# Coarse lag tables in two groups of eight shifts, and with that paired exponentials, weights multiplied before they are turned, and a new order

## The chip, the cores and the metric

The kernel runs on one core of one Trainium2 chip. A core has five engines that run on their own and meet only at semaphores: TensorE (PE, matmuls into PSUM), VectorE (DVE), ScalarE (ACT), GpSimd (POOL) and SyncE (SP, which here issues nearly all DMAs). Each engine works through its own list of instructions strictly in the order written. The metric is the device time of one execution in microseconds, the lower the better. It is not the span of the profile: the span runs from the first to the last instruction of the program, and some time lies around it.

## The reference, cut to what matters

```python
x = A_u                                            # [1, 2048, 512]
g = sigmoid((x * gate_w).sum(-1, keepdims=True))
# a: a state-space convolution over time, one filter of 2048 lags per channel d
dt = exp(log_dt)[:, None]
A, Bc, Cc = A_re + 1j*A_im, B_re + 1j*B_im, C_re + 1j*C_im      # [512, 128]
P = exp((dt*A)[:, :, None] * l)                    # l = 0..2047, as bf16
K = einsum("dn,dnl,dn->dl", Cc, P, dt*Bc).real
a = causal_convolution(x, K) + x * Dskip           # through FFTs of twice the length
# b: the two rows with the largest r go through a gated network and are added
r = x @ w_r;  idx = top2(r)
y = (silu(x[idx] @ w_gate) * (x[idx] @ w_up)) @ w_down * sigmoid(r[idx])
b = x + scatter(y, idx)
out = g * a + (1 - g) * b
```

## The kernel before, in words

**Tables.** Each lag is written as a sum of one of 32 coarse lags and one of 20 fine ones, so that exp(dt·A·l) is a product of two small tables. The coarse lags are 124 ± 4, 124 ± 12, and so on, which makes them the multiples of 8 from 0 to 248. The channels are handled in two halves of 256 (in the names the last digit, 0 or 1). For one half, `coarse` (L599) computes the decay part of the coarse table with one ACT exponential of 128x256 elements per coarse lag (`ep`, 32 per half) and the phases in four groups of four shifts. For a group, `phases` (L587) has PE build the angles in a PSUM tile of two banks (`pa`, lines 578 and 579, first 12 matmuls, then 4 more that turn the sine's argument into the cosine's), ACT takes a sine of 1024 elements after each of the two (`sin`), and DVE negates the sine (`ns`, L592). DVE then multiplies (`pi` and `pr`, 2048 elements each). The phase buffer `TRG` is there twice, so that two groups can be under way. `fine` (L822) has 20 exponentials per half (`eq`) and three groups of six DVE products (`px`, `py`, `s-`, `s+`, `qi`, `qr`), which also use the phases of the small shifts (`qargs`, made by PE in the same way, in two tiles) and of four larger ones (`args`, built by DVE or ACT at lines 559 and 560), and the weights C·B·dt.

**Weights.** The six parameter arrays arrive as [128, 512] (`nat0` to `nat5`), and PE turns each so that states lie on partitions (L509). For the weights, four turned arrays stand in PSUM; DVE copies two of them out (`cce`) and multiplies (`w1`, `w2`, `wr`, `wi`, then `kw` with dt).

**Lags.** For a half, `lags` (L841) contracts coarse and fine table over the 128 states: 128 matmuls of 80 columns (`kmm`, L853), moved out of PSUM in pieces of up to 960 elements (`kae`). 48 small matmuls with a selection matrix (`sel`, L868) put the wanted channels in place, 128 or 64 columns each, and one copy of 1280 elements (`kce`) makes the operand of the next step.

**Spectrum, products, inverse.** `spectrum` (L873) multiplies the filter with Fourier matrices (`ks`, lines 886, 888, 890 and 891; eight PSUM tiles per half, each moved out by one `khe` of 1024 elements). `transform` (L740) does the same for the input, in two blocks of time (`fw`, lines 724 and 727, moved out by `fwe` and `fwo`, combined by `vb`). `products` multiplies the two on DVE (`prod`, `acc`, `yr`, `yi`, `pq`; one part is summed on PE, `ac`, L936), and `inverse` transforms back (`iv`, lines 990 and 993) and scales with the gate while moving out (`ive`).

**Routing.** `log` (L615) gives the logits of all rows from a transposed load of the input (`xt`). A chain of small steps finds the two rows (`gm`, `gt`, L635), gathers them, runs the network (`ff`, `dn`) and writes the sum (`zt`, `z1`, `bu`, then an indirect write) into a copy of the input in memory, `u_routed`, which the inverse reads.

**Order.** Nothing is scheduled at run time. Every step is recorded with `P.add`, which also notes what it depends on through the buffers that it reads and writes, those that share memory with them, and PSUM tiles. `replay` then goes through `PLAN`, a written list of (step, engine choice), and through `BANKS`, the first PSUM bank of each tile; each engine gets its steps in that order. Some steps have a choice of engine, such as `fwe` or `kae` on ACT or DVE. A PSUM tile waits for everything that used its banks before. Line 376 is the helper of all DVE products, 392 of ACT copies, 398 of DVE copies, 401 of ACT functions. On SP the loads begin with the identity `cia`, `nat1`, `nat4`, `dga` (the first angles' matrices, 192 KB), `nat3`, `nat5`, the first half of the forward matrix `fm`, `nat2`, the first half of the input `u0`, `xt`, then `dgb` (the other angles' matrices, 576 KB) and `cf` (80 KB). On ACT the functions need two tables, one for exponentials and one for sines; each change is an ACT_TABLE_LOAD.

Around the change the order of half 0 and half 1 matters: `kmm` of half 0 begins at 64.9 us with four of its eleven steps, the rest follows at 81.5 us, after all of `transform` and of the phases of half 1.

Of the kernel before, what the change touches and what calls it, by code (L numbers as in the profile page):

```python
# [9 lines left out]
BF = mybir.dt.bfloat16  # L10
# [164 lines left out]
PLAN = [(0, 0), (4, 0), (5, 0), (3, 0), (6, 0), (1, 0), (23, 0), (29, 0), (225, 0), (2, 0), (13, 0), (7, 0), (180, 0), (22, 0), (244, 0), (207, 0), (243, 0),  # L175
# [126 lines left out]
def bass_gated_mix__ssm_conv_s4__moe_arch_mod__prompt_kernel(nc, A_u, A_A_re, A_A_im, A_B_re, A_B_im, A_C_re, A_C_im, A_log_dt, A_Dskip,  # L302
# [31 lines left out]
    with ExitStack() as es:  # L334
# [155 lines left out]
        for k, i in enumerate((2, 3, 4, 5)):  # L490
            nat(i, 2400.0 - 10 * k)
# [24 lines left out]
        for i in range(4):  # L516
            turned(2 + i, (tB, tC)[i // 2], i % 2)
# [604 lines left out]
```

## Time and profile before

| what | value |
|---|---|
| median of 3 runs | 169.99 us (169.45 to 170.62) |
| the profiled execution itself | 168.66 us |
| its span | 166.9 us, so 1.8 us lie around it |
| PE, DVE, ACT busy | 149.1, 146.0, 129.9 us |
| ACT_TABLE_LOAD | 7, 1.28 us each |
| granted TensorE clock, mean | 0.98 |

A busy PE is not PE at its peak, since the ends of its matmuls are modelled and overlap the next. For DVE and ACT a group's busy time divided by its count is close to the time from one start to the next when they follow each other. "Idle before" is time in which the engine stood still ahead of that instruction, put down to what released it.

### The profile page before, as it was taken

How to read it: one execution, taken by the hardware profiler on the slowest of the kernel's cores; microseconds unless marked ns; L12 is line 12 of the kernel's file. 1: busy time of each engine (PE TensorE's matmuls, PEld its weight loads, DVE VectorE, ACT ScalarE, POOL GpSimd, SP SyncE). 2: the span in 40 equal slices, each digit the busy share in tenths (PEclk: the TensorE clock that was granted, in tenths of full speed). 3: DMA queues.
4: the chain of work that ended last, by engine and by line, in shares of the span. 5: the costliest groups of instructions: out<-in, count | busy, mean ns of one | idle time of the engine just before them, and what ended most of it. 6: DMA issues, size and time to landing. Idle time of an engine off the chain costs nothing.

```text
span 166.9 us, 3538 instructions
## 1 busy us (share of the span) xinstructions
PE 149.1 (89%) x1483; PEld 108.0 (65%) x1491; DVE 146.0 (88%) x172; ACT 129.9 (78%) x243; POOL 17.9 (11%) x27
## 2 busy tenths in 40 slices
PE   1738998999999999999946899999999999999993
PEld 0523475666684685575633778768886785887882
DVE  0598899999998997898899999899897989999952
ACT  4599988999999999998999899698477360443432
POOL 6000000116005580000000042000000000000000
PEclk9975999999999999999999999999999999999999
DMA  3899999990009900001891000979300004001226
GB/s 113 300 356 230 265 389 374 415 377 18 1 9 335 602 4 0 4 0 29 277 401 51 2 4 24 338 298 370 110 0 0 4 0 126 0 4 55 70 70 181
DMA packets 21330, 25.89 MB, mean 155 GB/s; under 512 B 9118, under 2 KB 17188, under 8 KB 20644
## 3 DMA queue, kind: packets, MB, share of 16 engines
q1 hardware_dynamic: 21042, 25.55, 46.0%
q8 instruction: 11, 0.18, 0.4%
q10 hardware_dynamic: 146, 0.13, 0.2%
q0 software_dynamic: 128, 0.01, 0.2%
q14 instruction: 3, 0.02, 0.0%
HBM read 21.49 MB, written 4.20 MB: 154 GB/s over the span
## 4 chain that ended last, share of the span: by engine, by line
PE 62%; ACT 21%; DVE 7%; DMA 6%; SPq 2%; issue 1%
PE psm L993 17%; PE psm L724 12%; ACT RB L401 11%; PE psm L886 6%; ACT RB L392 6%; DVE RB L376 6%; DMA RB<-in_A_u_dram 6%; PE psm L936 4%; PE psm L853 3%; PE psm L578 3%; PE psm L579 3%; ACT L401 2%; PE psm L990 2%; PE psm L890 2%; PE psm L891 2%; PE psm L868 2%
## 5 line engine op out<-in xcount | busy, mean ns | idle before, releaser
L376 DVE TENSOR_TENSOR RB<-RB 128x2048 bf16<-128x2048 bf16 (+6 forms) x119 | 121.7, 1059 | 5.2 <-ACT RB L392 1.9
L392 ACT ACTIVATE RB<-psm 128x1024 bf16<-128x1024 f32 (+7 forms) x46 | 39.9, 908 | 12.3 <-PE psm L936 5.5
L401 ACT ACTIVATE RB<-RB 128x256 bf16<-128x256 f32 (+3 forms) x111 | 41.1, 452 | 2.3 <-DVE RB L376 2.3
L724 PE MATMUL psm<-RB 128*128 128x512 bf16 x121 | 31.7, 395 | 1.3 <-DMA RB<-in_A_u_dram 0.5
L993 PE MATMUL psm<-RB 128*128 128x256 bf16 x256 | 31.7, 273 | 0.0
L993 PEld LDWEIGHTS psm<-RB 128*128 128x128 bf16 x256 | 25.0, 98 | 3.1
L1007 ACT ACTIVATE RB<-psm,RB 128x256 bf16<-128x256 f32 x27 | 11.3, 472 | 16.6 <-PE psm L993 16.6
L401 ACT ACTIVATE RB<-psm 128x1024 bf16<-128x1024 int16 (+2 forms) x25 | 22.2, 936 | 0.6 <-PE psm L579 0.5
L724 PEld LDWEIGHTS psm<-RB 128*128 128x128 bf16 x128 | 12.6, 101 | 15.4 <-issue 2.2
L579 PE MATMUL psm<-RB 128*128 128x256 f16 x88 | 18.2, 273 | 0.3 <-ACT RB L401 0.3
L886 PE MATMUL psm<-RB 128*128 128x256 bf16 x128 | 16.3, 273 | 0.3 <-ACT RB L392 0.3
L578 PE MATMUL psm<-RB 128*128 128x256 f16 x88 | 15.0, 273 | 0.3 <-ACT RB L392 0.3
L853 PE MATMUL psm<-RB 128*128 128x80 bf16 x256 | 12.3, 199 | 2.5 <-ACT RB L392 1.6
L886 PEld LDWEIGHTS psm<-RB 128*128 128x128 bf16 x128 | 12.4, 98 | 2.1 <-ACT RB L392 0.6
L853 PEld LDWEIGHTS psm<-RB 128*128 128x128 bf16 x256 | 10.2, 97 | 4.9 <-PE psm L853 2.5
L401 ACT ACT_TABLE_LOAD x7 | 9.0, 1283 | 1.8 <-PEq L1107 1.7
L509 PE MATMUL psm<-RB 128*128 128x128 bf16 x24 | 5.4, 454 | 5.2 <-DMA RB<-in_A_B_re_dram 3.5
L578 PEld LDWEIGHTS psm<-RB 128*128 128x128 f16 x88 | 8.4, 98 | 2.5 <-ACT RB L392 0.4
L579 PEld LDWEIGHTS psm<-RB 128*128 128x128 f16 x88 | 8.2, 98 | 2.5 <-ACT RB L401 0.9
L398 DVE CAST RB<-psm 128x1024 bf16<-128x1024 f32 (+1 forms) x7 | 8.2, 1191 | 1.6 <-PE psm L853 1.1
L727 PE MATMUL psm<-RB 128*128 128x512 bf16 x31 | 9.3, 379 | 0.1
L990 PE MATMUL psm<-RB 128*128 128x256 bf16 x32 | 8.7, 273 | 0.2 <-issue 0.2
(64 smaller groups left out, 123.4 us busy)
## 6 DMA issues: line engine op xcount, KB each, us to landing
RB<-c_fwd SPq DMA_DIRECT2D x2, 1024.0 KB, 6.5
RB<-in_A_u_dram SPq DMA_DIRECT2D x2, 1024.0 KB, 9.4
RB<-c_near SPq DMA_DIRECT2D x2, 1024.0 KB, 5.1
RB<-c_inv SPq DMA_DIRECT2D x1, 2048.0 KB, 8.3
RB<-u_routed SPq DMA_DIRECT2D x2, 1024.0 KB, 6.8
RB<-in_B_w_gate_dram SPq DMA_DIRECT2D x1, 1792.0 KB, 9.9
RB<-in_B_w_up_dram SPq DMA_DIRECT2D x1, 1792.0 KB, 10.2
RB<-in_B_w_down_dram SPq DMA_DIRECT2D x1, 1792.0 KB, 7.5
```

The source lines that it names most:

```text
L376: return P.add(name, [(eng, c_dve(n, mode) if eng == DVE else 1.6, lambda h: h.tensor_tensor(out=o(), in0=a_(), in1=b_(), op=op))], rd, wr ...
L392: return lambda h: h.activation(out=o(), in_=a_(), func=ACTF.Copy, scale=scale() if callable(scale) else scale)
L401: return P.add(name, [(ACT, cost or c_act(n), lambda h: h.activation(out=o(), in_=a_(), func=func, scale=scale))], rd, wr, table=table, **kw)
L578: h.matmul(o, DGM(0, 128, (DPE.index(d) + 2) * 128, (1, 128)), HL(0, 128, k * 512 + c0, (1, w)), start=(k == 0 and i * w % 512 == 0), stop ...
L579: r = h.matmul(o, DGM(0, 128, 0, (1, 128)), DGM(0, 128, 128 + 1 - cs, (0, w)), start=False, stop=(cs == 0), skip_group_check=True)
L724: r = h.matmul(P32(t, k2, 0, 128, 0, (1, 512)), FM(0, 128, pl * 4096 + (par * 4 + q) * 512 + (2 * kp + k2) * 128, (1, 128)), U(0, 128, ((m ...
L727: r = h.matmul(P32(t, k2, 0, 128, 0, (1, 512)), CI(0, 128, 128 if pl == 1 - par * hc else 256, (1, 128)), V(0, 128, vo[0][2 * kp + k2] + ( ...
L853: x = h.matmul(P32(t, q // 6, 0, 128, (q % 6) * 80, (1, 80)), TPv(0, 128, ri * 16384 + c * 8192 + r * 128, (1, 128)), TQv(0, 128, c * 1024 ...
L886: x = h.matmul(o, KN(0, 128, g * 2048 + col, (1, 128)), KC[c](0, 128, g * 256, (1, 256)), start=(g == 0), stop=(g == NG - 1 and pl == 1))
L990: h.matmul(o, RD(0, 128, (tb + 8) % 16 * 128, (1, 128)), UE[qp](0, 128, (q2 * 2 + par) * 256, (1, 256)) if early else U2(0, 128, tb * D + ...
L993: x = h.matmul(o, G(0, 128, (pl * 4 + k0_ + kt) * 1024 + (par * 4 + q) * 128, (1, 128)), PQ(0, 128, 2048 * par + (k0_ + kt) * 512 + pl * 2 ...
L1007: r = h.activation(out=OT[k](0, 128, (4 * qp + 2 * q2 + par) * 256, (1, 256)), in_=P32(t, 0, 0, 128, q2 * 256, (1, 256)), func=ACTF.Copy, ...
```

## The change

- **Coarse groups.** `phases` is called twice per half with eight shifts instead of four times with four. The PSUM tile of the angles has four banks and always takes banks 4 to 7; a sine has 2048 elements; the products `pi` and `pr` have 4096. `TRG` is there once, in three parts (cosine, sine, negated sine), so a group's sine waits until `ns` and `pi` of the group before have read theirs, and its cosine until `pr` has.
- **Exponentials.** `exps` pairs a lag k with 2k: `doubled` has DVE write 2·dt·A (`al2`) and one ACT instruction with scale k reads dt·A and 2·dt·A, 512 elements, and writes both table columns. Of the 32 coarse lags of a half 20 are paired, of the 20 fine ones 12. Per half there are 22 and 14 exponentials in place of 32 and 20.
- **Weights.** `w1` and `w2` multiply the arrays as loaded, in SBUF; `wr` and `wi` follow, and PE turns the two results (`wt`, eight float32 transposes). `kw` reads them from PSUM. The 16 matmuls that turned the four arrays and `cce` are gone.
- **Small phases.** `qargs` of a half are made in one tile of three banks, 1536 elements per sine, in place of two tiles.
- **Lag selection.** `sel` has 16 matmuls of 320 columns, into four banks; `kce` puts the four interleaved parts together while it copies.
- **Order.** `PLAN` and `BANKS` are new, 499 steps in place of 569. What of it matters here: on SP the loads begin `dga`, `nat1`, `cia`, `nat3`, `nat2`, `cf`, `nat5`, `dgb`, `nat4`, `u0`, `fm`, `xt`. PE does the angles of the first group and `wt` ahead of the first `fw`. All of `transform` now stands ahead of `kmm` of half 0, and only the rest of the small phases of half 1 lies among the steps of that `kmm`. Between `sel` of half 1 and its spectrum stands `zt`, where one `iv` of the first inverse stood; that `iv` now follows the spectrum with the others. Two of seven `arg` steps stay on ACT, the other five go to DVE; `log` and `rs` go from ACT to DVE; one `kae` of half 0 and one of the copies of `fw` go from DVE to ACT. ACT changes its table eight times after the first load in place of six.

```diff
-        tB, tC = P.pst(2, "tb"), P.pst(2, "tc")
-        for i in range(4):
-            turned(2 + i, (tB, tC)[i // 2], i % 2)
-        EV("cce", row(CC, 0, 1024), lambda: P32(tC, 0, 0, 128, 0, (1, 1024)), [tC], [bCC], 1024)
-        TT("w1", row(W1, 0, 1024), pq_(tB, 0, 1024), row(CC, 0, 1024), ALU.mult, [tB, bCC], [bW1], 1024, 1)
+        TT("w1", row(W1, 0, 1024), lambda: NAT(0, 128, 1024, (1, 1024)), lambda: NAT(0, 128, 2048, (1, 1024)), ALU.mult, bNAT[2:], [bW1], 1024, 1)
...
+        tW = P.pst(2, "tw")
+        def wt(h):
+            r = None
+            for i, w in enumerate((W1, W2)):
+                for db in range(4):
+                    r = h.transpose(P32(tW, i, 0, 128, db, (4, 128)), w(0, 128, db * 128, (1, 128)), CF(0, 128, 0, (1, 128)))
+            return r
...
-        TRG = [at("TQ", 20480 + k * 6144, 6144, BF) for k in range(2)]
+        TRG = at("TQ", 20480, 12288, BF)
+        bTRG = [bf_("trg%d" % i, "TQ", 20480 + 4096 * i, 4096) for i in range(3)]
...
+        def doubled(hf):
...
+            TS("al2", lambda: ARF(0, 128, A2, (1, CW)), row(AL, hf * CW, CW), 2.0, ALU.mult, [bAL[hf]], [bA2[hf]], CW, 2)
+            return lambda: ARF(0, 128, a0, (A2 - a0, 2), (1, CW))
...
+        def exps(name, hf, mults, scale, out, step, buf):
+            left = list(mults)
+            while left:
+                k = left.pop(0)
+                two = [x for x in left if k and (x == 2 * k or k == 2 * x)]
+                if two:
+                    left.remove(two[0])
+                    k, k2 = min(k, two[0]), max(k, two[0])
+                    AF(name, lambda k=k, k2=k2: out(k, step(k2) - step(k)), AL2[hf], ACTF.Exp, [bAL[hf], bA2[hf]], buf(k, k2), 512, "exp", scale=k * scale, cost=0.52)
+                else:
+                    AF(name, lambda k=k: out(k, None), row(AL, hf * CW, CW), ACTF.Exp, [bAL[hf]], buf(k, k), 256, "exp", scale=k * scale, cost=0.31)
...
         def coarse(hf):
-            for u in range(4):
...
-                TT("pi", tp(1), tp(0), tr(2048, -1024), ALU.mult, [bTP[u][hf], bTRGc[k], bTRGn[k]], [bTPi[u][hf]], 2048)
-                TT("pr", tp(0), tp(0), tr(0, 0), ALU.mult, [bTP[u][hf], bTPi[u][hf], bTRGc[k]], [bTP[u][hf]], 2048)
+            for u in range(2):
+                phases(DP[8 * u:8 * u + 8], hf)
...
+                TT("pi", tp(1), tp(0), tr(4096, -2048), ALU.mult, [bTP[u][hf], bTRG[1], bTRG[2]], [bTPi[u][hf]], 4096)
+                TT("pr", tp(0), tp(0), tr(0, 0), ALU.mult, [bTP[u][hf], bTPi[u][hf], bTRG[0]], [bTP[u][hf]], 4096)
...
-            for us in ((0, 1), (2,)):
+            for us in ((0, 1, 2),):
...
-            t = P.pst(3, "sel")
+            t = P.pst(4, "sel")
...
-                for jp in range(3):
-                    nj = 2 if jp < 2 else 1
-                    for c4 in range(4):
-                        for g in range(4):
-                            x = h.matmul(P32(t, jp, 32 * g, 32, c4, (256, nj), (4, 64)), CI(0, 128, 384 + 32 * c4, (1, 32)),
+                for c4 in range(4):
+                    for g in range(4):
+                        x = h.matmul(P32(t, c4, 32 * g, 32, 0, (1, 320)), CI(0, 128, 384 + 32 * c4, (1, 32)),
...
-            EV("kce", lambda: KC[c](0, 128, 0, (1, 1280)), lambda t=t: P32(t, 0, 0, 128, 0, (1, 1280)), [t], [bKC[c]], 1280)
+            EV("kce", lambda: KC[c](0, 128, 0, (256, 5), (4, 64), (1, 4)), lambda t=t: P32(t, 0, 0, 128, 0, (64, 5), (1, 64), (512, 4)), [t], [bKC[c]], 1280)
```

More of the change, by code (lines that the diff above doesn't have):

```diff
@@ L410, in DMAT @@
             return P.add(name, [(SP, issue, lambda h: [h.dma_start_transpose(out=o(), in_=a_())])], [], wr, dma=(lat, kb / 250.0, 1), first=first)
[L413 removed]
+        AL = small("al", 2048, F32)[0]
+        bAL = [bf_("al%d" % i, "S", 1024 * i, 1024) for i in range(2)]
         BN, bBN = small("bn", 2048, F32)
@@ L587, in phases @@
         def phases(ts, hf):
-            k = nround[0] % 2
-            nround[0] += 1
-            pe_arg_sin(ts, lambda cs: (lambda: TRG[k](0, 128, 1024 * cs, (4, 4), (16, 64), (1, 4))), [bTRGc[k]], ((512, 4), (8, 64), (2, 4)), hf * CW, CW)
-            o_, a_ = row(TRG[k], 2048, 1024), row(TRG[k], 1024, 1024)
-            P.add("ns", [(DVE, c_dve(1024, 4), lambda h: h.tensor_scalar(out=o_(), in0=a_(), scalar1=-1.0, scalar2=None, op0=ALU.mult)), (ACT, c_act(1024), f_act(o_, a_, -1.0))], [bTRGc[k]], [bTRGn[k]])
@@ L593, in phases, with unit @@
-            return k
+            pe_arg_sin(ts, lambda cs: (lambda: TRG(0, 128, 2048 * cs, (4, 8), (32, 64), (1, 4))), lambda cs: [bTRG[cs]], ((512, 8), (8, 64), (2, 4)), hf * CW, CW)
+            o_, a_ = row(TRG, 4096, 2048), row(TRG, 2048, 2048)
+            P.add("ns", [(DVE, c_dve(2048, 4), lambda h: h.tensor_scalar(out=o_(), in0=a_(), scalar1=-1.0, scalar2=None, op0=ALU.mult)), (ACT, c_act(2048), f_act(o_, a_, -1.0))], [bTRG[1]], [bTRG[2]])
+        def unit(k):
+            return (15 - k if k < 16 else k - 16) // 8
```

61 lines of the change are left out of this document (33 added, 28 removed), and 69 rows, old and new, of the table PLAN.

## The prediction

> **What bounds the kernel now.** First the page, for who is busy and when.
>
> ```profile
> span 166.9 us, 3538 instructions
> PE 149.1 (89%) x1483; PEld 108.0 (65%) x1491; DVE 146.0 (88%) x172; ACT 129.9 (78%) x243; POOL 17.9 (11%) x27
> PE   1738998999999999999946899999999999999993
> ACT  4599988999999999998999899698477360443432
> PEclk9975999999999999999999999999999999999999
> ```
>
> Three engines are nearly full, so shares alone decide nothing. ACT is full up to about the middle and then thins out; PE shows its only holes at the start and in slices 21 and 22. The second view is busy time by stretch, cut where the chain of waits passes from ACT to PE.
>
> ```profile
> core 0: us, PE busy (x) PEld busy (x) DVE busy (x) ACT busy (x) POOL busy (x), PEclk, DMA share, GB/s
> 0.00:13.79 13.79, 5.96 (x25) 3.82 (x26) 6.82 (x13) 9.81 (x28) 2.69 (x8) 0.87 0.83 241
> 92.31:103.87 11.56, 11.25 (x105) 9.60 (x106) 11.25 (x14) 11.02 (x23) 2.87 (x1) 1.00 0.01 4
> 103.87:127.20 23.33, 22.73 (x308) 18.91 (x305) 20.26 (x17) 17.23 (x26) 0.00 (x0) 1.00 0.57 203
> 127.20:164.03 36.83, 36.58 (x303) 29.18 (x300) 33.39 (x33) 15.28 (x30) 0.00 (x0) 1.00 0.16 47
> ```
>
> ```profile
> 5.86:92.26 86.40, 76.19 (x767) 48.36 (x773) 79.96 (x109) 84.41 (x164) 12.39 (x18) 0.96 0.63 209
> ```
>
> From its first exponential to the first `kce` ACT stands still for 86.40 − 84.41 = 2.0 us; PE and DVE have more room there. From 103.87 to the last matmul PE stands for 0.9 us in 60.2. Between, the spectrum of half 0 needs PE for 11.25 of 11.56 us, and `kmm` of half 1 can't begin before DVE has the second fine table. The third view, the timeline around the first lag stage, shows the seam.
>
> ```profile
> 87.21 0.97 ACT L392 ACTIVATE RB<-psm 128x960 bf16<-128x960 f32 x1
> 88.23 2.69 PE L868 MATMUL psm<-RB 128*32 128x128 bf16 x48 [1.06 <-ACT RB L392]
> 91.03 1.22 ACT L392 ACTIVATE RB<-psm 128x1280 bf16<-128x1280 f32 x1
> 92.31 0.28 PE L890 MATMUL psm<-RB 128*128 128x256 bf16 x1 [1.39 <-ACT RB L392]
> 93.29 0.38 PE L697 MATMUL psm<-RB 128*2 128x128 bf16 x4
> ```
>
> PE waits for ACT's last `kae`, selects, waits for ACT's `kce`. So up to 92.3 us the end is set by the work that stands ahead of the last `kae` on ACT. DVE is the next bound, very close:
>
> ```profile
> 102.59 0.69 DVE L376 TENSOR_TENSOR RB<-RB 128x1024 bf16<-128x1024 bf16 x1
> ```
>
> This is the last product of the second fine table; it ends at 103.28, half a microsecond ahead of `kmm`.
>
> **The change on ACT, ahead of the last `kae` of half 0.** Groups of the stretch 5.86 to 92.26, ACT alone:
>
> ```profile
> L401 ACT ACTIVATE RB<-RB 128x256 bf16<-128x256 f32 x98 | 31.2, 404 | 2.3 <-DVE RB L376 2.3
> L401 ACT ACTIVATE RB<-psm 128x1024 bf16<-128x1024 int16 x20 | 19.3, 1022 | 0.6 <-PE psm L579 0.5
> L392 ACT ACTIVATE RB<-psm 128x1024 bf16<-128x1024 f32 x9 | 8.9, 1011 | 0.1
> ...
> L560 ACT ACTIVATE RB<-RB 128x512 int32<-128x512 f32 x7 | 4.1, 621 | 0.0
> ...
> L401 ACT ACTIVATE RB<-psm 128x512 bf16<-128x512 int16 x4 | 2.4, 591 | 0.0
> ...
> L392 ACT ACTIVATE RB<-psm 128x32 f32<-128x32 f32 x1 | 0.2, 198 | 1.0 <-PE psm L615 1.0
> ```
>
> *Exponentials.* One costs 31.2 / 98 = 0.318 us. No exponential of 512 is in the trace; sines say what 256 elements more cost, (1022 − 591) / 2 = 215 ns. A pair then takes 0.53 us in place of 0.64. Ahead of that `kae` stand 88 singles now, and 34 singles and 27 pairs after: 28.0 against 10.8 + 14.4, **−2.8 us**. The bounds are nothing saved (the pair reads two places far apart) and the 404 ns of one, which would be −6.
>
> *Phases.* Two sines of 1024 cost 2 x 19.3 / 20 = 1.93; one of 2048 costs 3.71 / 2 = 1.86 by the last row of the next fence. Eight such in place of sixteen, and four of 1536 in place of four of 1024 and four of 512 (0.965 + 0.6 against 0.965 + 0.43): −0.6 and −0.7. In a row of equal instructions each hides part of the one behind, and the short groups hide least, so I count a quarter, −0.3.
>
> *Moved steps.* Five `arg` leave ACT (5 x 4.1 / 7 = −2.9), `ns` too (−1.0, as a copy of 1024), `log` and `rs` with the wait of 1.0 (−1.3). Two more copies of `fw` (2 x 8.9 / 9 = +2.0) and one `kae` (+1.0) come, and two changes of table: +2.6. In the trace the sine behind a load begins at once, as the next rows show.
>
> ```profile
> 18.85 1.28 ACT L401 ACT_TABLE_LOAD   x1
> 20.14 3.71 ACT L401 ACTIVATE RB<-RB 128x2048 bf16<-128x2048 int16 x2
> ```
>
> The Trainium skill, "ScalarE: Activation LUTs", section "What ACT_TABLE_LOAD costs", gives a drain of about 1380 ns on top of each load of about 1283 ns. By that the two changes would cost 5.3 us and the sum below would turn from −1.7 to +1.0; the load's length agrees, but from its start to the next sine are 1.29 us, so the trace has no such drain.
>
> Sum on ACT: −2.8 − 0.3 − 2.9 − 1.0 − 1.3 + 2.0 + 1.0 + 2.6 = −2.7.
>
> *New waits of ACT.* The coarse phases become a chain without a spare buffer: PE 24 matmuls, sine, 8 matmuls, sine, and the next sine needs `ns`, `pi` or `pr` of the group before. Going down the new lists with these durations I find DVE ahead of each such sine by 1.4 us or more, and PE late for two: the cosine of the first group, behind two `fw` products that wait for the input, and that of the last, behind a `fw` of 2.6 us. The nearest row is the 0.5 us at L579 above, which the new waits replace. I take +0.7 more for both, between 0 and 4 (1 us for each of four groups). Left: **−2.0**.
>
> **The start on PE.** Ahead of the first `fw` the queue now carries `dgb` and `cf`, 656 KB more.
>
> ```profile
> RB<-c_diag SPq DMA_DIRECT2D x1, 576.0 KB, 4.3
> ```
>
> ```profile
> 13.79 6.98 PE psm L724 x24
> 34.71 1.73 PE psm L724 x8
> ```
>
> ```profile
> L635 PE MATMUL psm<-RB 128*128 128x128 f32 x8 | 1.6, 287 | 0.0
> ```
>
> In the first stretch 241 GB/s moved, so `fw` begins up to 2.7 us later, near 16. But PE then does in the gap what it did later, 24 angle matmuls (256 columns each, half of 1.73 / 8 = 0.216 us: 2.6 us) and eight turns in float32 (8 x 0.2 = 1.6 us, twice that on half clock). 16 turns are gone from a place where PE waited anyway. ACT meanwhile has its first exponentials and the phases of `transform`, which need no `u0`; it meets PE only near 20 us. So: nothing, with +1.5 as the upper bound, part of the waits above. `nat4` now lies behind `dgb`, and `w1`, `wt`, `kw` and the second `fw` behind `nat4`: another +1 at most, if it lands as late as 12 us.
>
> **DVE up to the second fine table.**
>
> ```profile
> L376 DVE TENSOR_TENSOR RB<-RB 128x2048 bf16<-128x2048 bf16 x74 | 88.0, 1219 | 4.2 <-ACT RB L392 1.9 <-ACT RB L401 1.5
> L376 DVE TENSOR_TENSOR RB<-RB 128x4096 bf16<-128x4096 bf16 x4 | 9.1, 2287 | 0.3 <-PE psm L936 0.2
> L559 DVE TENSOR_SCALAR RB<-RB 128x512 int32<-128x512 f32 x9 | 3.5, 418 | 0.0
> L398 DVE CAST RB<-psm 128x1024 bf16<-128x1024 f32 x4 | 4.8, 1218 | 0.5 <-PE psm L509 0.5
> L398 DVE CAST RB<-psm 128x960 bf16<-128x960 f32 x3 | 3.4, 1154 | 1.1 <-PE psm L853 1.1
> ```
>
> `pi` and `pr`: 16 x 1.19 against 8 x 2.28, −0.8. `cce`, one copy of `fw` and one `kae`: −1.2 − 1.2 − 1.1. Five `arg`: +1.9. Two `al2`, `log` and `rs`, no dearer than `arg`: +0.8 for all four. `ns` negates as many elements as before: nothing. `w1` and `w2` read bfloat16 from SBUF and still write float32: as before, at best half. `bu`, `rrec` and two reciprocals move behind: −0.7. Sum −2.3, so 101.0 us.
>
> **The lag stage and the tail.** The columns of `sel` stay (32 x 128 + 16 x 64 = 16 x 320); 48 starts become 16, and I take −0.4, between 0 and −0.9. `kce` reads across four banks; copies from PSUM cost by elements in all rows above, so 1.22, with double as the upper bound. `zt` (0.38) leaves the first spectrum: −0.3. `kmm` of half 1 then starts at 103.87 − 2.0 − 0.4 − 0.3 = 101.2, just behind DVE. Behind it the cover changes:
>
> ```profile
> 111.09 2.68 PE L868 MATMUL psm<-RB 128*32 128x128 bf16 x48
> 113.71 0.28 PE L990 MATMUL psm<-RB 128*128 128x256 bf16 x1
> 113.14 2.14 ACT L392 ACTIVATE RB<-psm 128x1024 bf16<-128x1024 f32 x2
> 115.69 0.27 PE L890 MATMUL psm<-RB 128*128 128x256 bf16 x1
> ```
>
> While ACT does the second `kce` (end of the third row), PE now does an `iv` from 113.71 to 115.69 that it needs anyway. After, only `zt` stands there, so PE waits about 1.2 + 0.2 − 0.3 = 1.1 us, does `zt` (+0.3) and saves 0.4 on `sel`: **+1.0**. From there to the end PE has the same matmuls. DVE has `bu` behind `zt` and `z1`, a stop of 1 to 2 us near 111; it has room for that, 33.39 of 36.83 us in the last stretch.
>
> **Sum.** −2.0 − 0.4 − 0.3 + 1.0 = −1.7 us: a span of 165.2, an execution of 168.66 − 1.7 = 167.0. That profiled execution lies 1.3 us under the median of the runs, so I take the difference over to the median: 169.99 − 1.7 = **168.3 us**, about 1% less, which is also about what a measurement of this kernel can tell from no change.
>
> **Rivals.**
> *The order gives more* (0.25): ACT's remaining stops vanish (the 2.0 us of the stretch in full) and the seam in the tail is covered. −1.7 − 2.0 − 1.0 = −4.7: 165.3. For it: with `log` gone the largest single stop of ACT is gone. Against it: DVE stands at 101.0, which leaves only 0.2 before it binds, so DVE too would have to lose waits.
> *The coarse chain binds* (0.18), the slower side: with one `TRG` and four banks held from the first angle matmul to the last sine, each of the four groups stops ACT by more than the 0.2 us I counted, because PE's 8 matmuls lie behind other products in PE's order. Price: 1.0 us per group gives +4.0 in place of +0.7, so 171.6; two `fw` in the way, 2 x 1.73 us, would make it more. From (0.7 + 1.7) / 4 = 0.6 us per group on the gain is gone. For it: every sine of a group passes PE twice. Against: none but one wait at L579 today.
> *PE falls to half clock* (0.06): in the unfilled lag stage PE idles more than now, and the first spectrum starts cold. In the fourth slice the granted clock is 0.5 and 24 matmuls take 6.98 us where 24 x 0.216 = 5.2 is the later pace: +1.8 per stage, two stages, 168.3 + 3.6 = 171.9. Against it: waits of 1.06 and 1.39 us in that stage left the clock at 1.00 in the stretch behind. The Trainium skill, "TensorE: Matmul & The Clock Gate", Part 1, has the clock halved after an idle window of about 3.4 us, which agrees with both.
> *The pairs do not save* (0.06): both halves cost as two, +2.8: 171.1.
>
> **How the numbers follow.** The forecast has 0.45. Faster by over 1% (under 168.3): half of it and the first rival, 0.46. Within 1%: the rest of it and mild cases of the second, 0.31. Slower by over 1% (over 171.7): the harder cases of the second and the third with small mishaps beside them, 0.23. The range goes from the first rival, 165.3, to the third with 0.4 for `kce`, 172.3.
>
> **What would show it.** Exponentials of 128x512 at 0.52 to 0.56 us each. Nine table loads. ACT's stops ahead of its first copy of 128x960 below 3 us in all. The first `ks` of half 0 near 89.6, `kmm` of half 1 near 101. A stop of PE of about 1 us ahead of the second spectrum. Wrong it would be if `kmm` of half 1 started after 103, if the first `fw` started after 17, or if `kce` were much over 1.2 us.

## The result and the profile after

The changed kernel takes **175.02 us** (median, 173.52 to 177.75) where the kernel before takes 169.72 beside it: a ratio of **1.028, 95% interval 1.022 to 1.034**. A repetition gave 175.49 and 1.031 (1.022 to 1.039). Forecast were 168.3 and a range of 165.3 to 172.3. The profiled execution took 173.52 us with a span of 171.4, against 168.66 and 166.9.

The page of after: its span, the busy time of the engines, and the rows of 40 slices for PE, ACT and the granted clock.

```profile
span 171.4 us, 3344 instructions
PE 150.1 (88%) x1419; PEld 106.5 (62%) x1419; DVE 145.7 (85%) x167; ACT 126.9 (74%) x194; POOL 31.1 (18%) x27
PE   1479995996899899999885699997999999999993
ACT  4599999998793999997989958574798471416061
PEclk9999999999759999999998799999999999999999
```

ACT has 3.0 us less to do in all (129.9 before), as intended, and yet the end is later. Two things are new in the row of the clock: it falls in slices 11 and 12, and again in 22 and 23. Before, it fell only in slices 3 and 4. The busy time by stretch says where the time went; the columns are start and end, length, then busy time and instructions of PE, PEld, DVE, ACT and POOL, the granted clock, the DMA share and GB/s.

```profile
core 0: us, PE busy (x) PEld busy (x) DVE busy (x) ACT busy (x) POOL busy (x), PEclk, DMA share, GB/s
5.50:95.81 90.31, 77.95 (x738) 48.33 (x736) 79.17 (x101) 82.58 (x117) 15.88 (x10) 0.95 0.64 215
95.86:106.83 10.97, 10.77 (x96) 9.37 (x96) 10.49 (x13) 8.44 (x14) 0.00 (x0) 0.99 0.18 76
106.83:118.22 11.39, 9.66 (x156) 6.32 (x157) 10.52 (x10) 7.27 (x10) 6.09 (x8) 1.00 0.01 3
118.22:168.50 50.28, 50.04 (x424) 41.27 (x424) 44.99 (x44) 26.57 (x54) 6.42 (x2) 1.00 0.27 87
```

The first row ends with the first `kce`. ACT's first exponential in it starts at 6.22 us, where it started at 5.86:

```profile
6.22 7.89 ACT L396 ACTIVATE RB<-RB 128x256 bf16<-128x256 f32 x21 [2.66 <-DVE RB L371]
```

ACT is busy for 82.58 us of the row where it was busy for 84.41 before, so its work fell by 1.8. But from its first exponential on it now stands still for 95.81 − 6.22 − 82.58 = 7.0 us instead of 2.0. The first `kce` ends 3.6 us later (95.81 against 92.25), and the first spectrum matmul comes at 95.86 (before 92.31, forecast 89.6). `kmm` of half 1 starts at 106.83 (forecast 101.2). Before, its row starts at 103.71; the 103.87 of the prediction is the end of the matmul ahead of it.

```profile
103.71 6.17 PE L853 MATMUL psm<-RB 128*128 128x80 bf16 x128
```

What ACT waited for is seen on PE. First PE's timeline, then ACT's and DVE's rows that answer to it.

```profile
39.79 1.46 PE L746 MATMUL psm<-RB 128*128 128x512 bf16 x6
43.41 0.25 PE L682 MATMUL psm<-RB 2*128 2x2 bf16 x4 [2.16 <-DMA RB<-in_A_u_dram,RB]
43.59 1.06 PE L586 MATMUL psm<-RB 128*128 128x256 f16 x8
44.49 1.60 PE L694 MATMUL psm<-RB 128*128 128x2 bf16 x56
45.95 1.87 PE L746 MATMUL psm<-RB 128*128 128x512 bf16 x4
47.61 1.06 PE L749 MATMUL psm<-RB 128*128 128x512 bf16 x2
48.46 1.91 PE L746 MATMUL psm<-RB 128*128 128x512 bf16 x4
50.17 1.06 PE L749 MATMUL psm<-RB 128*128 128x512 bf16 x2
```

```profile
43.69 0.18 ACT L387 ACTIVATE RB<-psm 128x8 bf16<-128x8 f32 x1 [1.34 <-PE psm L682]
44.69 1.88 ACT L396 ACTIVATE RB<-psm 128x2048 bf16<-128x2048 int16 x1 [0.30 <-PE psm L586]
54.21 1.88 ACT L396 ACTIVATE RB<-psm 128x2048 bf16<-128x2048 int16 x1 [2.80 <-PE psm L586]
```

```profile
69.76 2.89 DVE L371 TENSOR_TENSOR RB<-RB 128x4096 bf16<-128x4096 bf16 x2 [5.02 <-ACT RB L396]
```

PE comes to `gat`, the matmul on the two gathered rows, and waits 2.16 us for the gather. Behind it come eight angle matmuls and 56 matmuls of two columns. Then the ten products of 512 columns from 45.95 to 50.17 take 0.42 us each, twice their 0.216. ACT pays for both: 1.34 + 0.30 us at the gather, and 2.80 ahead of the first sine of half 1, whose angles PE did only after the slow products. DVE pays next, with 5.02 us ahead of the first coarse product of half 1. From there its chain stays late up to the second fine table.

Last, the seam in the tail.

```profile
106.83 6.18 PE L876 MATMUL psm<-RB 128*128 128x80 bf16 x128 [0.21 <-DVE RB L371]
114.23 2.65 PE L889 MATMUL psm<-RB 128*32 128x320 bf16 x16
116.69 0.41 PE L719 MATMUL psm<-RB 128*2 128x128 bf16 x4
118.22 1.92 PE L907 MATMUL psm<-RB 128*128 128x256 bf16 x16 [1.13 <-ACT RB L387]
```

From `kmm` of half 1 to the end of the last matmul are 168.50 − 106.83 = 61.67 us, where they were 164.03 − 103.71 = 60.32: +1.35.

### The profile page after: what moved, and what is told of

It reads as the page before. It is cut to its first block, busy times and chain, and to the rows that moved or that the text cites. A ratio compares the mean times of both kernels' runs of the same rounds, so it can differ in the third digit from the quotient of the medians.

```text
span 171.4 us, 3344 instructions
## 1 busy us (share of the span) xinstructions
PE 150.1 (88%) x1419; PEld 106.5 (62%) x1419; DVE 145.7 (85%) x167; ACT 126.9 (74%) x194; POOL 31.1 (18%) x27
## 4 chain that ended last, share of the span: by engine, by line
PE 62%; ACT 21%; DVE 7%; DMA 5%; issue 2%; SPq 0%; DVEq 0%
PE psm L1014 16%; ACT RB L396 15%; PE psm L746 10%; PE psm L907 6%; ACT RB L387 5%; DVE RB L371 5%; PE psm L749 5%; PE psm L957 4%; DMA RB<-in_A_u_dram,RB 4%; PE psm L586 4%; PE psm L889 3%; PE psm L585 3%; PE psm L876 3%; PE psm L1011 2%; PE psm L911 2%
## 5 line engine op out<-in xcount | busy, mean ns | idle before, releaser
L387 ACT ACTIVATE RB<-psm 128x1024 bf16<-128x1024 f32 (+6 forms) x48 | 42.8, 917 | 17.5 <-PE psm L957 5.7
L396 ACT ACTIVATE RB<-RB 128x256 bf16<-128x256 f32 (+3 forms) x79 | 38.4, 561 | 2.7 <-DVE RB L371 2.7
L746 PE MATMUL psm<-RB 128*128 128x512 bf16 x128 | 33.0, 395 | 1.6 <-ACT RB L387 1.6
L396 ACT ACTIVATE RB<-psm 128x2048 bf16<-128x2048 int16 (+2 forms) x13 | 21.4, 1647 | 3.8 <-PE psm L586 3.6
L1028 ACT ACTIVATE RB<-psm,RB 128x256 bf16<-128x256 f32 x25 | 10.0, 477 | 15.8 <-PE psm L1014 15.8
L586 PE MATMUL psm<-RB 128*128 128x256 f16 x88 | 19.1, 286 | 1.2 <-ACT RB L396 1.2
L585 PE MATMUL psm<-RB 128*128 128x256 f16 x88 | 17.3, 302 | 3.2 <-DVE RB L371 3.2
L585 PEld LDWEIGHTS psm<-RB 128*128 128x128 f16 x88 | 9.4, 109 | 6.6 <-DVE RB L371 3.6
L375 POOL TENSOR_SCALAR RB<-RB 128x28 bf16<-128x28 bf16 (+3 forms) x4 | 3.9, 962 | 50.9 <-ACT RB L396 50.8
L876 PE MATMUL psm<-RB 128*128 128x80 bf16 x256 | 11.8, 199 | 0.9 <-DVE RB L371 0.2
L586 PEld LDWEIGHTS psm<-RB 128*128 128x128 f16 x88 | 8.7, 103 | 3.8 <-ACT RB L396 2.1
L749 PE MATMUL psm<-RB 128*128 128x512 bf16 x32 | 10.4, 411 | 0.0
L377 POOL TENSOR_SCALAR RB<-RB 128x1 f32<-128x1 f32 (+2 forms) x3 | 4.9, 1623 | 25.4 <-DVE RB L658 25.2
```

The source lines that it names most:

```text
L387: return lambda h: h.activation(out=o(), in_=a_(), func=ACTF.Copy, scale=scale() if callable(scale) else scale)
L396: return P.add(name, [(ACT, cost or c_act(n), lambda h: h.activation(out=o(), in_=a_(), func=func, scale=scale))], rd, wr, table=table, **kw)
L585: h.matmul(o, DGM(0, 128, (DPE.index(d) + 2) * 128, (1, 128)), HL(0, 128, k * 512 + c0, (1, w)), start=(k == 0 and i * w % 512 == 0), stop ...
L586: r = h.matmul(o, DGM(0, 128, 0, (1, 128)), DGM(0, 128, 128 + 1 - cs, (0, w)), start=False, stop=(cs == 0), skip_group_check=True)
L746: r = h.matmul(P32(t, k2, 0, 128, 0, (1, 512)), FM(0, 128, pl * 4096 + (par * 4 + q) * 512 + (2 * kp + k2) * 128, (1, 128)), U(0, 128, ((m ...
L749: r = h.matmul(P32(t, k2, 0, 128, 0, (1, 512)), CI(0, 128, 128 if pl == 1 - par * hc else 256, (1, 128)), V(0, 128, vo[0][2 * kp + k2] + ( ...
```

## The experiments

The theory from the two traces: the operations of the change cost about what was priced, but in the new order PE comes to the gather too early, stands still, and loses its clock. The rivals: the coarse chain with its one buffer binds, or the new operations are dearer than priced.

### PE kept busy at the gather

`filler10`: matmuls that nobody reads, ahead of `gat`. `filler5` has five of them.

```diff
+        tf = P.pst(1, "fil")
+        def fil(h):
+            r = None
+            for _ in range(10):
+                r = h.matmul(P32(tf, 0, 0, 128, 0, (1, 512)), CI(0, 128, 0, (1, 128)), CI(0, 128, 128, (1, 512)), start=True, stop=True)
+            return r
+        MM("fil", fil, [bCIA, bCIB], [tf], 2.160)
         tg = P.pst(1, "gat")
```

> After with ten matmuls of 128x512 that nobody reads put on PE between the eighth product of the first transform and the matmul on the gathered rows (a bank that is free there; the result is unchanged). They fill the 2.16 us for which PE stood still ahead of that matmul. Theory A (the changed order puts nothing else on PE there, the stop halves the clock, and the next twelve products of 512 columns take 0.427 us each instead of 0.216): the matmul on the gathered rows stays at 43.4, PE's clock row shows 9 in all slices, the twelve products take 2.6 us instead of 5.1, ScalarE's wait of 2.80 ahead of the sine at 54.21 goes, half 0's first spectrum matmul comes at 93.3 instead of 95.86, the profiled execution is 2.2 to 3.0 below after's 173.52, so 170.5 to 171.3. Rival B (the clock fell for another reason, or the delay is hidden by ScalarE's and VectorE's slack): 173 to 174, no change.

> As filler10 with five such matmuls, so that a stop of about 1.1 us stays ahead of the matmul on the gathered rows. If a stop of some 2 us is what the clock answers to: as filler10, clock full, 170.5 to 171.3. If the thin stretch behind it (56 matmuls of two columns over 1.5 us) counts as much: the twelve products are slow again and the time is 173 to 174.

`filler10` took 172.73 us, ratio 1.016 (1.005 to 1.027). Its PE at the gather:

```profile
41.45 2.32 PE L683 MATMUL psm<-RB 128*128 128x512 bf16 x10
43.76 0.25 PE L690 MATMUL psm<-RB 2*128 2x2 bf16 x4
44.84 1.54 PE L702 MATMUL psm<-RB 128*128 128x2 bf16 x56
46.45 0.81 PE L754 MATMUL psm<-RB 128*128 128x512 bf16 x3
```

`gat` starts no earlier than in after, yet the products behind it run at full pace, and ACT's 2.80 us are gone. The first spectrum matmul comes at 93.30, as expected. So the half clock came from the stop. But the profiled execution took 172.99 us where 170.5 to 171.3 were expected, because the clock now fell at another place. The rows give PE's busy time, its instructions and its clock in the first spectrum, first of `filler10`, then of `fill_all`, which is told below.

```profile
94.00:98.00 4.00, 4.00 (x22) 0.53 0.37 156
```

```profile
94.00:98.00 4.00, 4.00 (x37) 1.00 0.45 193
```

In `filler10` only 22 matmuls got through in those 4 us. The stops of PE ahead of `sel` and ahead of the first `ks` (2.23 and 1.34 us) cost it its clock there. After has the same two stops, and its clock falls there too (slices 22 and 23), but in the profiled execution it is back when the spectrum starts.

`filler5`, a single execution, took 176.02 us. A stop of 1.48 us was left ahead of `gat`, and the clock fell behind it again, and also near 31, where PE waits ahead of a product of the first transform. So its expectation fell on the side of the thin stretch: a stop of 1.5 us with 56 matmuls of two columns behind it was enough in this execution.

### The gather replaced by an early load

```diff
-        DMA("gu", lambda h: [h.indirect_dma_start(GU(0, 2, 0, (1, D)), None, rows_u, bass.IndirectOffsetOnAxis(ap=IDX(0, 2, 0, (1, 1)), axis=0))], [bIDX], [bGU], ...)
+        DMA("gu", lambda h: [h.dma_start(GU(0, 2, 0, (1, D)), dr(A_u, 0, (D, 2), (1, D)))], [], [bGU], ...)
```

> After with the gather of the two routed rows replaced by a plain load of the first two rows, issued on the same queue some 10 us earlier: the routed computation works on other rows than the reference's, everything else is as it was. The matmul on the gathered rows waits no longer for a transfer. Theory A: the whole cost of that transfer is the clock (as in filler10, 2.2 to 3.0) plus the 2.16 us wait itself, of which ScalarE, the engine behind, has 1.3 to 2 back: first spectrum matmul of half 0 near 91.6, profiled execution 168.5 to 169.7, level with before's 168.66. Rival B (ScalarE and the coarse chain bind, not PE): 172 to 174.

170.94 us, ratio 1.004 (0.998 to 1.011): between the two expectations, and nearer the first. The wait is gone and the clock is full at the products behind `gat`, but in the profile it fell near 31 and in the lag stage instead.

### The changed kernel again, one pair exchanged, and all stops filled

`gat_swap` puts the eight angle matmuls ahead of `gat`; the numbers are steps of the order. It changes a second thing, which its expectation does not name: the copy of the gathered rows (step 79) goes from ACT to DVE.

```diff
-(107, 0), ... (78, 0), ... (79, 1), ... (197, 0),
+(107, 0), ... (197, 0), (78, 0), (79, 0),
```

`fill_all` has matmuls that nobody reads at all four places where PE stands still: 6, 10, 10 and 7.

> The changed kernel once more, unaltered, beside the other three. If the clock falls behind stops of PE of two microseconds and more, wherever they are, its profile shows the fall behind the stop at the gathered rows (41 to 43) and may show it behind those at 28 to 31 and at 89 to 96 as well; time 172.5 to 176, moving with the number of falls.

> After with one pair exchanged in PE's order: the eight angle matmuls that stand behind the matmul on the gathered rows go ahead of it. The stop of 2.16 us there becomes one of at most 0.9 between them and the gathered rows (the eight take 0.88, the sine behind them starts 1.9 us earlier). Theory: the twelve products behind run at 0.216, ScalarE's 2.80 at 54 goes, first spectrum matmul of half 0 near 93; 170.5 to 172.8 (the upper end where the clock still falls behind the stops at 89 to 96). Rival (any stop ahead of the thin 56 matmuls is enough, as in filler5): products at 0.427 again, 173 to 175.

> After with matmuls of 128x512 that nobody reads in all four stops of PE: six ahead of the product that starts near 30, ten ahead of the matmul on the gathered rows, ten ahead of the selecting matmuls of half 0, seven ahead of the first spectrum matmul of half 0. No work is moved, no wait is taken away, only PE stays busy. Theory: the clock row shows 9 from the fifth slice on, no product of 512 or 256 columns takes twice its time, and the 2.2 us that the half clock cost filler10 in the spectrum (93.3 to 97.7) come back: profiled execution 169.8 to 171.5, 2 to 3.5 below after on the same chip; what is left above before is waits and the tail. Rival (the clock falls for power or on its own): still falls, 172.5 and more.

`fill_all`: **171.61 us, ratio 1.010 (1.007 to 1.013)**, beside 175.49 of the changed kernel. The clock rows of `after_again` and `fill_all`:

```profile
PEclk9999999699969699999999699999999999999999
```

```profile
PEclk9999999999999999999999999999999999999999
```

Nothing was moved and no wait taken away, so the **half clock costs about 3.9 us** (175.49 − 171.61), nearly three quarters of the loss (175.49 against 170.12 of the kernel before beside it). The executions tell the same; the mean granted clock stands beside the time.

| kernel | clock and time of single executions |
|---|---|
| after_again | 0.970: 174.1; 0.960: 175.4, 175.5; 0.961: 176.2 |
| gat_swap | 0.978: 171.9, 172.1; 0.968: 173.1; 0.970: 173.7; 0.961: 176.1; 0.951: 177.3 |
| fill_all | 1.000: 171.2, 171.4, 171.4, 171.6, 171.6, 171.7, 171.7; 0.999: 171.6; 0.998: 172.2; 0.989: 173.1 |

`gat_swap` (173.39, ratio 1.017, 1.009 to 1.025) shortens the stop about as expected, and its executions lie in the ranges of the theory and of the rival, and above both. Its profile, of its slowest execution, has a stop of 1.02 us and then half the pace all the same:

```profile
45.33 0.25 PE L683 MATMUL psm<-RB 2*128 2x2 bf16 x4 [1.02 <-DMA RB<-in_A_u_dram,RB]
45.83 1.55 PE L695 MATMUL psm<-RB 128*128 128x2 bf16 x56 [0.26 <-DVE RB L391]
47.25 1.86 PE L747 MATMUL psm<-RB 128*128 128x512 bf16 x4
```

The Trainium skill, "TensorE: Matmul & The Clock Gate", Part 1, has the clock judged over free-running windows of about 3.4 us. That the same kernel falls at one place in one execution and at another in the next agrees with it. So do the lengths: in all 19 traces every stretch at half clock between its start and its end lasts 3.41, 6.83 or 10.24 us, which is one, two or three times 3.41. That a stop of about 1 us with thin work around it can be enough is what these runs add.

Does the kernel before lose its clock in its own lag stage too? `before_fill` fills its three stops there, in the same way.

> The kernel before with 7, 4 and 6 matmuls of 128x512 that nobody reads in the three stops that PE has in half 0's lag stage (1.57, 1.06 and 1.39 us in its profile), nothing else changed. Executions of the kernel before lie between 168.3 and 171.7 with granted clocks from 1.00 to 0.96, so it too seems to lose its clock in some of them. If it loses it there: clock 0.98 or more in all executions and 168.3 to 169.5. If it loses it elsewhere or not by idling: as before, 169.1 to 171.7.

169.76 us, ratio 0.999 (0.995 to 1.002): no gain. Its stops of 1.06 to 1.57 us cost nothing that can be measured. What a fall of the clock costs depends on where it comes: executions of the kernel before with a mean clock of 0.959 took 169.3 to 171.5 us, those with 0.98 took 168.5 to 171.7.

### The wait alone, and the pairs alone

With the clock out of the way two prices can be read. `fill_plain` is `fill_all` with the early load; `fill_unpaired` is `fill_all` with two exponentials of 256 columns in place of each pair, the edit that `unpaired` makes to the changed kernel.

```diff
-                    AF(name, lambda k=k, k2=k2: out(k, step(k2) - step(k)), AL2[hf], ACTF.Exp, [bAL[hf], bA2[hf]], buf(k, k2), 512, "exp", scale=k * scale, cost=0.52)
+                    def two_(h, k=k, k2=k2):
+                        h.activation(out=out(k, None), in_=row(AL, hf * CW, CW)(), func=ACTF.Exp, scale=k * scale)
+                        return h.activation(out=out(k2, None), in_=row(AL, hf * CW, CW)(), func=ACTF.Exp, scale=k2 * scale)
+                    P.add(name, [(ACT, 0.62, two_)], [bAL[hf], bA2[hf]], buf(k, k2), table="exp")
```

> After with every paired exponential issued as two of 256 columns in the same place. Theory: a pair costs ScalarE 0.52 start to start and two singles 2 x 0.306 = 0.61; 27 pairs ahead of the first spectrum of half 0 make +2.5 on ScalarE, less what its waits (6.6 us of them up to there) take up; 174.5 to 176.5, 1 to 2.5 above after. Rival (the doubled exponents save nothing because ScalarE waits anyway): within 0.5 of after's 173.52.

> fill_all with the plain early load of two fixed rows in place of the gather (the routed computation works on other rows than the reference's), and so without the ten matmuls that fill that stop. The clock is full in both, so the difference to fill_all's 171.6 is the wait for the gather alone: ScalarE has 1.51 + 0.30 us of stops from it in fill_all. Theory: 1.0 to 1.8 less, 169.8 to 170.6. Rival (ScalarE's stop is made up for by its later waits of 0.4 to 0.7): within 0.4 of 171.6.

> fill_all with every paired exponential issued as two of 256 columns. With the clock out of the way this prices the pairs alone: 27 of them ahead of half 0's first spectrum, 0.09 each, so 2.0 to 2.5 more on ScalarE, which stands on the path up to there; 173.2 to 174.1. Rival (VectorE is the bound there and takes it up): 171.6 to 172.3.

`unpaired` gave 176.24 us (173.77 to 179.51), ratio 1.022 (1.011 to 1.033). In its profile the clock fell in four places (slices 8, 12, 14 to 15 and 23), and the spread hides the price. `fill_unpaired` gives 173.69, ratio 1.021 (1.014 to 1.028), so the **pairs save about 2 us**: 2.1 by the medians (173.69 − 171.61), 1.8 by the two ratios, since the kernel before was 0.16 us faster beside it. `fill_plain` gives 170.32, ratio 1.002 (0.998 to 1.006), so the **wait for the gather costs 1.3 us** beyond the clock by the medians. The clock was not full in all executions, though: five of the ten of `fill_plain` have 0.988 to 0.99 and took 170.8 to 171.3 us, the other five 0.999 or more and 169.0 to 169.9. Full clock against full clock (medians 169.56 and 171.6) the wait costs 2.0.

### The same operations in another order

`fill_plain` is level with before, not 1.7 us below it. Is the rest the operations' own, or their order's?

`order_front` moves many steps up to the second lag stage.

> After with the same operations, the same tiles and banks in another order up to the second lag stage (ten evictions and angle steps change between ScalarE and VectorE; the gathered rows' matmul, the turn of the kernel's zero lag and the products of the second transform stand where their inputs are there). Theory: the operations of the change are cheap enough, the loss lay in the order that came with them. With no stop of PE over 1.6 us after 14 and ScalarE and VectorE waiting for 1 to 2 us in all, the first spectrum matmul of half 0 comes near 88.5 and the lag matmuls of half 1 near 99.5: profiled execution 166 to 168, below before. Rival (the coarse chain with one table buffer or the wider operations themselves bind): 170 and more, with ScalarE or VectorE waiting ahead of the coarse products.

174.94 us, ratio 1.028 (1.021 to 1.035): a miss. The order had a fault of its own. On ACT a sine went ahead of nine exponentials, and each such change of function loads a table:

```profile
28.42 1.45 ACT L397 ACTIVATE RB<-psm 128x1536 bf16<-128x1536 int16 x1
29.89 1.28 ACT L397 ACT_TABLE_LOAD   x1
31.18 3.84 ACT L397 ACTIVATE RB<-RB 128x256 bf16<-128x256 f32 x8
```

```profile
33.56 2.29 DVE L372 TENSOR_TENSOR RB<-RB 128x4096 bf16<-128x4096 bf16 x1 [4.09 <-ACT RB L397]
```

DVE waited 4.09 us for those exponentials, and PE 5.70 us behind DVE; it says nothing on the operations.

`order_new` and `order_new_fill`:

> After with the same operations in another order from 16 us on (the search for the two routed rows, the gather and the products behind it earlier on VectorE and PE, three evictions of the second transform and of the lag stage on the other engine), tiles and banks as in after. order_front had crowded ScalarE between 20 and 33; here that stretch holds what it held in after. Theory (the operations of the change are worth what was priced and the loss lay in their order): no stop of PE over 1.6 us behind 16, so a full clock; first spectrum matmul of half 0 near 89.2 to 90.2, lag matmuls of half 1 near 100.4 to 101.4, tail as in after (66 us from there to the end of the execution): 167 to 168.5, below before. Rival (the coarse chain or the wider operations bind whatever the order): 169.5 and more, with ScalarE or VectorE waiting over 3 us in all between 30 and 90.

> order_new with six matmuls of 128x512 that nobody reads in each of the two stops of PE in half 0's lag stage. If those stops (about 1.4 us each) still cost the clock in some executions: 0.5 to 1.5 below order_new with a narrower spread; if not: the same within 0.4.

179.53 us, ratio 1.057 (1.050 to 1.064), and 180.56, ratio 1.064 (1.055 to 1.072). They are no test either. In both, a bank was handed to another tile between the two halves of an inverse sum, and a weight load had gone ahead of the input `u1`.

`order_b` keeps the early loads in place.

> After with the same operations, tiles and banks and the same order of the transfers, in another order of the engines' steps between 16 us and the end (some twenty places; eleven evictions and angle steps change engine). order_new had a bank taken by another tile between the two halves of a sum, and had moved input loads; neither is done here. The gathered rows arrive when they do in after, near 43.3, but PE has the last product of the first transform and the angle matmuls ahead of them. Theory (part of the loss is the order's): no stop of PE over 1.6 us behind 16, first spectrum matmul of half 0 near 91 to 92, lag matmuls of half 1 near 102 to 103.3; 169 to 170.4, level with before, as fill_plain. Rival (the last two microseconds are the new operations' own): 171 to 172, as fill_all.

> order_b with six matmuls of 128x512 that nobody reads in each of the two stops of PE in half 0's lag stage. If those stops (about 1.4 us each) cost the clock in some executions: 0.5 to 1.5 below order_b with a narrower spread; if not: the same within 0.4.

174.64 us (ratio 1.022, 1.014 to 1.030) and 171.25 (1.011, 1.006 to 1.016): both above what was expected, and the fillers gained 3.4 us where at most 1.5 was expected. The front came as forecast, with the first spectrum matmul at 91.61 and `kmm` of half 1 at 102.66, but the tail lost it. PE's wait ahead of an inverse product, and the DMA issues that explain it:

```profile
125.69 3.62 PE L958 MATMUL psm<-RB 128*128 128x512 bf16 x16
132.02 0.27 PE L1012 MATMUL psm<-RB 128*128 128x256 bf16 x1 [2.72 <-ACT RB L388]
132.12 1.76 PE L1015 MATMUL psm<-RB 128*128 128x256 bf16 x8
```

```profile
124.00 0.37 SPq L1078 DMA_DIRECT2D RB<-u_routed  x1
124.41 2.63 SPq L1060 DMA_DIRECT2D RB<-u_routed  x4
```

Against what its expectation says of the transfers, a long load (L1078, 1 MB) had gone ahead of the four short ones (L1060) that the product needs. The view names ACT as releaser; `order_c`, where those loads come first again, has no such wait. The clock fell behind the stop: nine matmuls of 256 columns from 132.02 to 133.68, 0.18 us each.

`order_c` puts that back, and takes the turn of the routed rows (`zt`) to the first spectrum, where the kernel before had it. Its order on PE around the gather, in step names:

```diff
-fw/T0  gat  pa/C0  ff  fw/T1  pa/C1  ff  pa/C1  fw/T1  dn
+fw/T0  pa/C0  gat  ff  pa/C1  ff  fw/T1  pa/C1  fw/T1  dn
-sel/L1  zt  ks/S1
+sel/L0  zt  ks/S0
```

Beside that, one `kae` of each half and some smaller steps are on DVE in place of ACT, and some tiles have other banks.

> order_b with two things mended: the turn of the routed rows (with its two evictions, the add and the scatter) goes back from behind half 1's selection to the first spectrum, as in the kernel before, and the two short loads of the routed rows go ahead of the long ones again. order_b lost 2.9 us at 129 to the wait for them, and its clock behind it; its front had come as forecast (first spectrum matmul 91.61, lag matmuls of half 1 102.66). Theory: that wait is gone, the rest stays: 169.0 to 170.6. Rival (the two microseconds are the operations' own, and come back elsewhere): 171 and more.

> order_c with six matmuls of 128x512 that nobody reads in each of the two stops of PE in half 0's lag stage: full clock from 16 us on, 168.8 to 170, level with before or below it; the rival as for order_c.

**169.14 us, ratio 0.999 (0.996 to 1.003)**, and 169.29 with the fillers, ratio **0.998 (0.995 to 1.0004)**. With the operations of the change and no work left out, that is 5 to 6 us below after, and no measurable distance from before. Without the fillers the clock still falls in some executions: seven of the twelve took 168.6 to 169.2 us, five 170.8 to 171.4, and the profile of one of the five has slice 7 at half clock. Three rows of PE in `order_c_fill`, the first `ks` of half 0, `kmm` of half 1 and the first `ks` of half 1:

```profile
91.38 1.91 PE L918 MATMUL psm<-RB 128*128 128x256 bf16 x16
101.96 6.14 PE L887 MATMUL psm<-RB 128*128 128x80 bf16 x128
113.46 1.92 PE L918 MATMUL psm<-RB 128*128 128x256 bf16 x16 [1.35 <-ACT RB L388]
```

The first two come 0.9 and 1.75 us ahead of before's (92.31 and 103.71). The third row, the second spectrum, is 2.2 us ahead of before's 115.69, but before had done an inverse product of 2 us by then, which here still lies behind. That is where the lead goes.

## Why the prediction was wrong

**The step that failed is "New waits of ACT", +0.7 between 0 and 4.** Measured are +5.0 (7.0 against 2.0). The step followed each sine of the coarse chain back to DVE and PE, and did not ask what PE itself would wait for. In the new order PE is free for `gat` at 41.25, where it came to it at 46.50, but the index of the gather ends only 1.7 us earlier (36.49 against 38.23). The trace of before has the index on DVE, `gat` on PE, and the gather's time from issue to landing (the last number):

```profile
38.03 0.20 DVE L389 SCALAR_TENSOR_TENSOR RB<-RB 2x1 int32<-2x1 f32 x1
45.11 1.03 PE L724 MATMUL psm<-RB 128*128 128x512 bf16 x4
46.50 0.25 PE L660 MATMUL psm<-RB 2*128 2x2 bf16 x4
```

```profile
RB<-in_A_u_dram,RB POOLq DMA_INDIRECT x1, 3.9
```

PE was busy until 8.3 us behind the index, so a gather of 3.9 us was never waited for. In after the gather itself is slower:

```profile
RB<-in_A_u_dram,RB POOLq DMA_INDIRECT x1, 6.6
```

It was issued at 36.81. With 3.9 it would have landed at 40.7, ahead of PE; with 6.6 it landed at 43.4, and PE stood still for 2.16 us. So the price in the trace of before alone would not have shown the wait. In `order_b`, `order_c` and `order_c_fill` the gather takes 3.9 to 4.0 again, but there PE has other work for 6.8 to 6.9 us behind the issue, so 6.6 would have been covered as well. What slows it was not tested alone. It goes with POOL's own instruction, 5.46 us in after, 2.84 in before and 2.77 in `order_c`. In 16 of the 17 traces with a gather that instruction ends 0.9 to 1.1 us behind the first break in DVE's row of instructions; in after the row runs from 36.41 to 41.29, in before up to 40.50, two microseconds behind the issue. That DVE's work holds the gather up is thus argued, not shown.

**The rival "PE falls to half clock"** had 0.06 and a price of 3.6 us, for two lag stages. It is what happened, at 3.9 us in the median, but spread over the input, the gather and the lag stage. That the two prices are close is chance, since they are for different places. Its reason against, that waits of 1.06 and 1.39 us had left the clock full, holds for the kernel before, as `before_fill` shows; it does not carry over to other stops with thin work around them.

**The work on ACT fell by 1.8 us, where the sum had 2.7.** The single prices were about right. The groups of ACT from the first exponential to `kce`:

```profile
L396 ACT ACTIVATE RB<-RB 128x512 bf16<-128x512 f32 x29 | 16.7, 620 | 0.0
L396 ACT ACTIVATE RB<-psm 128x2048 bf16<-128x2048 int16 x8 | 15.0, 1877 | 3.7 <-PE psm L586 3.6
L396 ACT ACTIVATE RB<-RB 128x256 bf16<-128x256 f32 x38 | 13.5, 405 | 2.7 <-DVE RB L371 2.7
L396 ACT ACT_TABLE_LOAD x8 | 10.3, 1283 | 0.1
```

In a row of equal ones a pair starts 0.52 us behind the last, as forecast (0.53), and a single 0.31, so two singles are 0.61, not 0.64. 27 pairs then save 2.5 instead of 2.8, and about 2 show in the time. The sines of 2048 take 1.88 (1.86). A table load costs its 1.28 and no drain: one starts at 46.66 and the function behind it at 47.96. The rival that pairs do not save is out. Where the rest of the missing 0.9 went is open.

**The coarse chain does not bind.** Of the 3.6 us that ACT waits for angles at L586, 2.80 stand behind the half-clock products; the rest is 0.8 over four groups, 0.2 each as forecast, and of this 0.30 was counted at the gather above.

**The start on PE** was right: the first `fw` starts at 15.28 (near 16), and no wait of ACT follows from it.

**DVE's second fine table** came at 106.8, not 101.0, but not by its own work: the 5.02 us from 64.74 to 69.76 are ACT's delay passed on. The same wait is 2.23 in `fill_all` and 0.44 in `fill_plain`. In `order_c_fill` `kmm` of half 1 starts at 101.96, 0.8 behind the forecast 101.2.

**The lag stage.** `kce` is 1.24 us (1.22). `sel` of half 1 takes 116.69 − 114.23 = 2.46, where it took 2.62: −0.16, not −0.4. Sixteen starts instead of 48 save little.

**The tail** is +1.35, not +1.0. The stop is 1.13 us as forecast (1.1); the missing part is `sel` (0.24) and the 0.41 of `zt`, priced at 0.3. The prediction's own sign of being wrong, `kmm` of half 1 after 103, came at 106.83.

**The sum, rebuilt.** The forecast was −1.7 and the medians differ by +5.3, so 7.0 us are to be explained. The half clock is 3.9 of them and the wait for the gather 1.3 to 2.0, which leaves 1.1 to 1.8. The pairs (about 2 in place of 2.8), `sel` of half 0 (0.24) and the tail (0.35) make about 1.3. The sum of operations was too hopeful by about that: in the best order found the kernel takes 169.1 to 169.3, a change of −0.1 to −0.4 by the ratios, and neither interval reaches the −1.0% that was forecast. The order that came with the change was not that one.

## What to carry to other kernels

When an order changes, follow each engine's queue for what it will wait on, transfers too, and compare the time from issue to landing with the work that is left to cover it; a wait that never showed may only have been covered. That time can change with the order too: 3.9 us before, 6.6 after. A stop of PE costs more than its length, since the matmuls behind it may run at half pace for several microseconds: look at the row of the clock first when a kernel is slower with less work. Matmuls that nobody reads, put into PE's stops, separate the two prices in one run.

## What the runs showed of the hardware

- The clock falls behind much shorter stops than expected: behind 2.16 us in after, and in one execution each behind 1.48 us (`filler5`) and 1.02 us (`gat_swap`), both with 56 matmuls of two columns next to them. In the kernel before, stops of 1.57, 1.06 and 1.39 us within 8 us left it at 1.00. Length alone does not decide, and the same kernel falls at different places in different executions.
- The gather of two rows of 1 KB took 6.6 us from issue to landing in after, 3.9 in before and 3.9 to 4.0 in `order_b` and `order_c`. What made the difference was not tested alone.
- Not settled: what the gather waits for in after, and whether an inverse product could again cover the second `kce`. It would need DVE's products of half 0 earlier, and wasn't tried.
